# Last five groups of heads in two visits, their weights parked in DRAM, MLP operands made inside the attention

## Chip, cores, metric

One core of a Trainium2 chip. The metric is the device time of one execution in microseconds. All data is float32; matrix products are made of float32r parts (a high part, and a low part that is the rest).

## The reference

```python
x = A_x                                               # 1 x 2048 x 576
mod = (silu(c) @ w_mod)                               # six rows of 576: sa, ca, ga, sb, cb, gb
h = layernorm(x) * (1 + ca) + sa
# attention: 32 query heads of 128, 16 key/value groups, the last 512 cached positions
q = (h @ wq); p = softmax(q @ k.T * 128 ** -0.5); o = p @ v
x = x + ga * (o @ wo)                                 # wo: 4096 x 576
h = layernorm(x) * (1 + cb) + sb
gate, up = h @ W_gate, h @ W_up                       # 576 x 4608 each
x = x + gb * (((gate * (gate > 0)) * up) @ W_down)
```

## The kernel before

The 2048 tokens are four blocks of 512 (`qb` 0 to 3), kept transposed in `hT`. The attention runs over 128 **units**. A unit is one query head on one block of tokens: `unit(u)` gives group `g`, block `qb` and head; a group of two heads takes eight units in a row (four blocks by two heads), with the group's keys and values (`ks`, `vs`) and the heads' `wqs` and `wos` in SBUF.

In unit `u` the scores (`s_half`, L408 to L410) are followed on TensorE by the query projection of the next unit (`qproj`, L361), by `spread` (L436), by a piece of the output product (`piece`, L537), by the two halves of probabilities times values of the unit before (`pv_half`, L510 to L512), and by another piece. VectorE (DVE) reduces the scores to a maximum (L413, L421), adds up the exponentials' sums of the unit before (`sum_pre`, L428), broadcasts the maximum (L466), subtracts it (L483), broadcasts the inverse sum (L446), makes the low part of the next query (`q_lo`, L392) and scales the unit's output (`o_mul`, L518). ScalarE (ACT) makes the exponentials (L485), their high parts (L472), the high parts of outputs and weights, and copies the running sum into PSUM and back (L570, L546). GpSimd (POOL) makes the low parts of the exponentials (`lo_half`, L492, two per unit), their sums over keys (`ksum_op`, L498 and L501, three instructions per unit), the low part of the output (`o_lo`, L526) and of weights (`split`, L176). `spread` sends maximum and sum in one matmul, so it needs both L422 and L428.

All engines issue in the order in which the program is written. Work beside the units is put at a time by `step(name, t, fn)`: `t` is ten times the unit plus a place in it, and `run(u, k)` issues what is due at place `k` of unit `u` (`PLAN` adds a shift to some names, `CFG` picks engines of a layernorm). `prep` puts the load of a weight, its gate (`wo` is multiplied by the row `ga`, L216 on DVE) and its split at such times. `prep_mod` adds up the modulation rows (L127 on DVE).

`LayerNorm` takes a block of 512 tokens: statistics on DVE, scaling on ACT, transposes on TensorE (L306), an affine step, and for the MLP (`key == "b"`) a store to DRAM (`hb`). The MLP works on two halves of 1024 tokens (`b` 0 and 1), 18 blocks `m` each, in a scheme with seven products in place of eight: P1 to P7 with sums of weights (`wop`) and of tokens (`hop`: B11, B21, T1 to T4, B22). `w_prep` makes the weights of the first half and keeps them in DRAM (`wkeep`), from which the second half loads them. `md_piece` is the down product (L537), `ln_half` the second half's layernorm inside the first half's blocks, `h_later` its token operands, kept in `hkeep` and loaded by `h_back`. The first half's layernorms (`b0`, `b1`), token operands (`h_steps`) and first weights are made at the end of the attention, at times from `e - 41` to `e + 4`, where `e` is the end of unit 127.

Of the kernel before, what the change touches and what calls it, by code (L numbers as in the profile page):

```python
# [26 lines left out]
PLAN = {'a1.st0': -14, 'a1.nm0': -15, 'a1.st1': -14, 'a1.nm1': -15, 'a1.st2': -14, 'a1.nm2': -15, 'a1.st3': -14, 'a1.nm3': -15, 'a1.rs': -15, 'a1.tr0': -15, 'a1.af0': -11, 'a1.tr1': -15, 'a1.af1': -15, 'a1.tr2': -15, 'a1.af2': -15, 'a2.tr2': -1, 'wo2.g': 2, 'a3.st0': -10, 'a2.st2': -10, 'wq2.c': 4, 'wo2.l': -2, 'wo2.c': -2, 'mods': -3, 'k1.l': -5, 'k1.c': -8, 'gb': -12}  # L27
CFG = {'a3': (('m', 'aav', 'vap'), ('w', 'vvv', 'aav'), ('w', 'vvp')), 'a2': (('m', 'aav', 'vvv'), ('w', 'vvv', 'vvv'), ('s', 'aap')), 'a0': (('s', 'vvp', 'vvv'), ('m', 'aap', 'avp'), ('w', 'aav')), 'a1': (('w', 'aap', 'vap'), ('m', 'vvp', 'vvv'), ('s', 'avp'))}
PE0, PE1, MLP0 = 4, 3, 8


@with_exitstack
def kernel(
# [96 lines left out]
    def prep_mod(j, t):  # L130
        st = {}

        def load():
            st["raw"] = rp.tile([P, 640], F32, tag="raw", name=f"wm{j}_{t}")
# [71 lines left out]
    def prep_out(d, k, src, key, slot=None, at=(None, "wC")):  # L206
# [11 lines left out]
        def cut():  # L218
            raw = st["gated"]
            w = d[slot] = wp.tile([P, 2, D], F32R, tag=at[1], name=f"wo{key}_{k}")  # L220
            split(raw, D, w[:, 0, :], w[:, 1, :])
# [11 lines left out]
    def hb_store(qb, d, cols, f):  # L233
        if d < 4:
            nc.sync.dma_start(hb[qb, d][:, cols], f)
            return
        for j in range(2):
            s = f[32 * j:32 * j + 32]
            nc.sync.dma_start(hb[qb, 4][j, :, :, cols].rearrange("r p n -> p r n"),
# [17 lines left out]
    class LayerNorm:  # L257
        def __init__(self, qb, key, where):
            self.qb, self.key, self.where = qb, key, where
            self.xn, self.ps, self.ready, self.n = {}, {}, 0, 0  # L260
# [21 lines left out]
        def norm(self, i):  # L282
            pool, tag, w = self.where[i]
            n = pool.tile([P, w], F32, tag=tag, name=f"xn{self.key}_{self.qb}_{i}",
                          **({"bufs": 2} if tag == "lo" else {}))
            a = acc[4 * self.qb + i]
            act = dict(bias=self.rs[:, 1, i:i + 1], scale=self.rs[:, 0, i:i + 1])
            nc.scalar.activation(n[:, :512], a[:, :512], AF.Identity, **act)
            nc.scalar.activation(n[:, 512:640].rearrange("p (r n) -> p r n", r=2),
                                 a[:, None, 512:].to_broadcast([P, 2, 64]), AF.Identity, **act)  # L290
            self.xn[i] = n
            assert adds[4 * self.qb + i] == (HQ // 2 if self.key == "b" else 0)

        def trans(self, ds, pool, tag):
            nm = f"lt{self.key}_{self.qb}_{ds[0]}"
            if tag == "w":
                flush()
            if tag != "mm":
                t = pool.tile([P, 2, 512], F32, tag=tag, name=nm)
            for j, d in enumerate(ds):  # L300
# [4 lines left out]
                for i in range(4):  # L305
                    nc.tensor.transpose(self.ps[d][:, i * P:(i + 1) * P],  # L306
                                        self.xn[i][:, d * P:(d + 1) * P], ident)

        def affine(self, ds, pool, tag, engs):
            qb = self.qb  # L310
            if self.key == "b":
                add, mul = mods["b"]
                for d, e in zip(ds, engs):
# [7 lines left out]
                    hb_store(qb, d, slice(0, 512), f[:n])  # L321
                return
            if not self.ready:
                hT[qb] = [hp.tile([P, 512], F32R, tag="hT", name=f"hT{self.key}_{qb}_{k}")
                          for k in range(9)]
            h = hT[qb]
            self.ready += len(ds)
# [36 lines left out]

    NU = HKV * NQB * 2
    wqs, ks, vs, wos = {}, {}, {}, {}
# [3 lines left out]
    def unit(u):  # L370
        g, r = divmod(u, 2 * NQB)
        qb, hh = divmod(r, 2)
        return g, qb, 2 * g + hh
# [154 lines left out]
    def down_piece(his, los, ws, i, qt, nm, pool=None, seed=None):  # L528
# [3 lines left out]
        for half in range(2):  # L532
            cs = slice(half * H2, (half + 1) * H2)
            n = 0
            for hi, lo, w in zip(his, los, ws):
                for a, b in ((hi, 0), (hi, 1), (lo, 0)):
                    nc.tensor.matmul(ps[:, half, :H2], a[:, sl], w[:, b, cs],  # L537
# [68 lines left out]
    def order(m):  # L606
        return ("P1", "P6", "P2", "P7", "P5", "P4", "P3") if m else ("P1", "P2", "P6", "P7", "P5", "P4", "P3")
# [15 lines left out]
    def lay_steps():  # L623
        out = []
        for f in range(0, NFT, 2):
            for xx, src in enumerate((wg, wu)):
                for j in range(2):
                    out.append((wlay[f:f + 2, j, :, xx, 0:256], src[f:f + 2, :, 256 * j:256 * j + 256]))
        for f in range(0, NFT, 9):
# [696 lines left out]
```

## Time and profile before

| | |
|---|---|
| median of three runs | 3063.35 us (3063.14 to 3064.06) |
| profiled execution | 3058.63 us, span 3056.8 us, mean granted clock 0.982 |
| busy | PE 95%, PEld 83%, DVE 66%, POOL 65%, ACT 44% |
| DMA | 360.28 MB, mean 118 GB/s |

PE is TensorE's matmuls, PEld its weight loads, SP the engine that issues most of the DMAs. In a row of the timeline stand start, length, engine, line, operation, what is written and read, shapes, and in brackets the engine's idle time ahead of it and what ended it. "x2" is two instructions in one row. The slices are 40 equal parts of the span, in tenths.

### The profile page before, as it was taken

What the parts mean: (1) busy time and instruction counts of PE and PEld (TensorE: products, weight loads), DVE (VectorE), ACT (ScalarE), POOL (GpSimd) and SP (SyncE); (2) the same over time, 40 slices, a digit from 0 to 9 for tenths busy, and PEclk for the clock granted to TensorE, in tenths of its full rate; (3) what the DMA queues carried; (4) which work ended last, traced back from release to release, by engine and by line L of the source; (5) the groups of instructions that cost most, each with busy time, mean ns of one, the idle gap of its engine ahead of it and who ended that gap; (6) DMA issues with size and microseconds to landing.
All of it is one profiled execution on the core that took longest, in us unless ns stands there. A gap on an engine that the chain in (4) does not pass through costs nothing. (4 is left out here: it accounts for less than half of the span.)

```text
span 3056.8 us, 40707 instructions
## 1 busy us (share of the span) xinstructions
PE 2914.2 (95%) x15414; PEld 2533.1 (83%) x15414; DVE 2027.2 (66%) x2810; ACT 1360.2 (44%) x1875; POOL 1988.1 (65%) x1386
## 2 busy tenths in 40 slices
PE   6899999999999999999987699999999999999999
PEld 4688888888888888888875488888878888888888
DVE  7777777777777777777765656566767444444444
ACT  5566666666666666666653233333323111111110
POOL 5789899998998999898975556666666311111111
PEclk9999999999999999999998799999999999999999
DMA  4101111211111100000003256567777944444443
GB/s 146 39 23 50 66 62 63 73 58 55 47 43 51 34 24 28 16 16 21 25 29 99 107 210 218 212 222 273 267 273 252 346 162 161 162 164 162 175 161 116
DMA packets 143651, 360.28 MB, mean 118 GB/s; under 512 B 12768, under 2 KB 52448, under 8 KB 143456
## 3 DMA queue, kind: packets, MB, share of 16 engines
q1 hardware_dynamic: 115312, 245.15, 24.4%
q10 hardware_dynamic: 28144, 112.54, 9.3%
q8 instruction: 122, 2.00, 0.3%
q14 instruction: 73, 0.60, 0.1%
HBM read 234.62 MB, written 151.32 MB: 126 GB/s over the span
## 5 line engine op out<-in xcount | busy, mean ns | idle before, releaser
L492 POOL TENSOR_TENSOR lo<-p,hi 128x1024 fp32r<-128x1024 f32 x256 | 610.1, 2404 | 0.1
L864 PE MATMUL gu<-hop_T,wop 128*128 128x512 f32 (+1 forms) x2016 | 507.1, 396 | 18.3 <-ACT hop_T L714 11.1
L537 PE MATMUL md<-wogb,hhi 128*128 128x288 f32 x2304 | 477.0, 299 | 40.3 <-ACT lflh L849 16.2
L548 DVE TENSOR_TENSOR acc<-md,acc 128x576 f32<-128x576 f32 x288 | 217.5, 755 | 408.3 <-PE md L537 408.1
L413 DVE TRANSPOSE_TENSOR_REDUCE t<-s 128x32 f32<-128x1024 f32 x256 | 319.2, 1248 | 226.2 <-PE s L410 212.7
L537 PEld LDWEIGHTS md<-wogb,hhi 128*128 128x128 f32 x2304 | 389.3, 191 | 71.1 <-DVE acc L548 20.7
L864 PEld LDWEIGHTS gu<-hop_T,wop 128*128 128x128 f32 (+1 forms) x2016 | 372.7, 190 | 91.1 <-ACT hop_T L714 12.0
L537 PE MATMUL wo<-woga,ohi 128*128 128x288 f32 x2048 | 428.6, 302 | 13.2 <-DVE acc L548 8.5
L361 PE MATMUL qps<-hTa,wA 128*128 128x512 f32 x1792 | 431.8, 392 | 4.7 <-POOL hTa L349 3.5
L361 PEld LDWEIGHTS qps<-hTa,wA 128*128 128x128 f32 x1792 | 338.4, 189 | 76.5 <-POOL hTa L349 4.4
L501 POOL TENSOR_TENSOR ks<-ks,p 128x512 f32<-128x512 f32 x256 | 340.4, 1330 | 79.7 <-ACT p L485 65.2
L864 PE MATMUL gu<-hop_B,wop 128*128 128x512 f32 (+1 forms) x1512 | 382.9, 396 | 4.7 <-DVE hop_B L718 3.6
L537 PEld LDWEIGHTS wo<-woga,ohi 128*128 128x128 f32 x2048 | 333.6, 190 | 26.7 <-DVE acc L548 10.1
L880 POOL TENSOR_TENSOR hlo<-r,hhi 128x512 fp32r<-128x512 f32 x72 | 100.8, 1400 | 384.8 <-issue 240.8
L537 PE MATMUL md<-wogb,hlo 128*128 128x288 f32 x1152 | 343.6, 298 | 0.6 <-POOL hlo L880 0.6
L864 PEld LDWEIGHTS gu<-hop_B,wop 128*128 128x128 f32 (+1 forms) x1512 | 281.8, 191 | 62.3 <-DVE hop_B L718 4.0
L537 PE MATMUL wo<-woga,olo 128*128 128x288 f32 x1024 | 302.8, 296 | 0.1
L483 DVE TENSOR_TENSOR p<-s,mb 128x1024 f32<-128x1024 f32 x242 | 285.0, 1219 | 3.8
L472 ACT CAST hi<-p 128x1024 fp32r<-128x1024 f32 x256 | 269.2, 1052 | 8.0
L485 ACT ACTIVATE p<-p 128x1024 f32<-128x1024 f32 x242 | 255.5, 1056 | 5.5 <-POOL kv L176 4.9
L879 ACT CAST hhi<-r 128x512 fp32r<-128x512 f32 x72 | 44.7, 621 | 416.8 <-DVE r L889 334.9
L537 PEld LDWEIGHTS md<-wogb,hlo 128*128 128x128 f32 x1152 | 219.6, 191 | 1.4 <-POOL hlo L880 1.4
(180 smaller groups left out, 5292.9 us busy)
## 6 DMA issues: line engine op xcount, KB each, us to landing
wk_P<-wop ACTq DMA_DIRECT2D x126, 640.0 KB
wop<-wk_P SPq DMA_DIRECT2D x126, 640.0 KB
wr<-wlay SPq DMA_DIRECT2D x72, 384.0 KB
dk<-wogb ACTq DMA_DIRECT2D x36, 576.0 KB
wogb<-dk SPq DMA_DIRECT2D x36, 576.0 KB
rogb<-wd SPq DMA_DIRECT2D x36, 288.0 KB
rwA<-wq SPq DMA_DIRECT2D x32, 320.0 KB
wlay<-wg SPq DMA_DIRECT2D x36, 256.0 KB
```

Of the source, the lines that this page charges most:

```text
L361: return [lambda i=i, a=a, b=b: nc.tensor.matmul(ps, a, b, start=(i == 0), stop=(i == n - 1)) for i, (a, b) in enumerate(ops)]
L413: nc.vector.tensor_reduce(t4[u][:, 2 * h:2 * h + 2, :].rearrange("p k b -> p (k b)"), t.rearrange("p k (b j) -> p (k b) j", j=32), axis=AX ...
L472: nc.scalar.copy(hi_[u, h], pt[u, h])
L483: nc.vector.tensor_tensor(p, t, bc[u][:, None, :].to_broadcast([P, 2, 512]), op=ALU.subtract)
L485: nc.scalar.activation(p, p, AF.Exp, bias=0.0, scale=1.0)
L492: nc.gpsimd.tensor_sub(lo_[u, h], pt[u, h], hi_[u, h].bitcast(F32))
L501: nc.gpsimd.tensor_tensor(ks_[u], ks_[u], p[:, j, :], op=ALU.add)
L537: nc.tensor.matmul(ps[:, half, :H2], a[:, sl], w[:, b, cs], start=(n == 0 and seed is None), stop=(n == 5), skip_group_check=seed is not None)
L548: nc.vector.tensor_tensor(av, ps[:, :, :H2], av, op=ALU.add)
L864: nc.tensor.matmul(ps, a, c, start=s not in ("P2", "P3") and i == 0, stop=i == len(ops) - 1, skip_group_check=True)
L879: nc.scalar.copy(hi, r)
L880: nc.gpsimd.tensor_sub(lo, r, hi.bitcast(F32))
```

## The change

- The units are listed: groups 0 to 10 as before, then groups 11 to 15 with blocks 0 and 1 (units 88 to 107), then the same groups with blocks 2 and 3 (units 108 to 127). Pieces of the output product keep their regular times up to the end.
- The weights of groups 12 to 15 are split during groups 1 to 8 (`parks`) and stored in DRAM (`keep`, issued by ACT). Those of group 11 are stored after their first use. `again` loads them for each visit; every other odd `wo` is kept in two `raw` buffers.
- The first of the three sums of a unit goes from POOL to DVE, behind `q_lo`; `lo_half(u, 0)` stands right after the exponentials, and the other two sums stand after the copy of the high part.
- Splits of the groups' weights get new times (-30, -20, -14, 0, 20, 34 from the visit's begin `B`).
- The layernorms `b0` and `b1` run in units 108 to 117 with buffers of `hp`; the token operands of the first half are made in units 114 to 126 (`h0_load`, `h0_comb`, `h0_cut`), kept in `hkeep` and loaded by `h_back`.
- The seven weights of block 0 are made in units 24 to 84 on POOL (`w_later`) and loaded like those of the second half.
- `ln_half` transposes two and two columns in place of four; in `w_prep` the next block's loads are issued behind its own work; modulation rows go through the pool `xm`; the entries of `PLAN` and `CFG` for the layernorms `a2` and `a3`, the second group's weights and `gb` go.

```diff
-PLAN = {..., 'mods': -3, 'k1.l': -5, 'k1.c': -8, 'gb': -12}
+PLAN = {..., 'mods': -3}
+NLAST = 5
...
+    def keep(key, t):
+        akeep[key] = k = dr.tile(list(t.shape), F32R, name="ak%s%d" % key)
+        nc.scalar.dma_start(k.bitcast(F32), t.bitcast(F32))
...
+    VIS = [(g, (0, 1, 2, 3)) for g in range(HKV - NLAST)]
+    VIS += [(g, (0, 1)) for g in range(HKV - NLAST, HKV)] + [(g, (2, 3)) for g in range(HKV - NLAST, HKV)]
+    UNITS = [(g, qb, 2 * g + hh) for g, qbs in VIS for qb in qbs for hh in range(2)]
...
             ks_[u] = xp.tile([P, 512], F32, tag="xm", name=f"ks{u}")
-            nc.gpsimd.tensor_tensor(ks_[u], p[:, 0, :], p[:, 1, :], op=ALU.add)
+            nc.vector.tensor_tensor(ks_[u], p[:, 0, :], p[:, 1, :], op=ALU.add)
...
+        if m % NFP == 0 or m >= NFP:
+            nc.sync.dma_start(w_tile(n).bitcast(F32), wkeep[m % NFP, s].bitcast(F32))
             return
...
+    def h0_cut(s, x, t):
+        a, n = h0[(*x, t)], 96 if t == 2 else P
+        hi = hp.tile([P, 512], F32R, tag="hT", name=f"hy0_{s}_{t}")
+        nc.scalar.copy(hi[:n], a[:n])
+        if t < 2:
+            lo = hp.tile([P, 512], F32R, tag="hT", name=f"hz0_{s}_{t}")
+            nc.gpsimd.tensor_sub(lo, a, hi.bitcast(F32))
...
+    H = 10 * UNITS.index((HKV - 1, 1, HQ - 1))
+    norm_steps("b0", 0, "b", None, None, (H + 16, H + 20, H + 26, H + 29), H + 30,
+               (H + 34, H + 36, H + 44, H + 46), (H + 48, H + 58, H + 68), (H + 49, H + 59, H + 69), www)
...
+            for (key, d, pr), t in zip(weights(g, live), (-30, -20, -14, 0, 20, 34)):
+                prep(key[0] + str(key[1]), B + t, pr, 3)
...
+        for c, t in (("q", 10), ("kv", 26), ("o", 44)):
+            if parks[c]:
+                key, d, pr = parks[c].pop(0)
+                prep("park", B + t, pr, 3)
+                sk(B + t + 9, key, d, key[1])
...
         exp_half(u, 0)
-        ksum_op(u, 0)
         flush()
         run(u, 5)
         exp_half(u, 1)
-        ksum_op(u, 1)
+        lo_half(u, 0)
         if u:
             sum_bc(u - 1)
...
             piece(at[10 * u + 6])
+        ksum_op(u, 0)
         run(u, 7)
...
         flush(pend_act)
-        lo_half(u, 0)
+        ksum_op(u, 1)
         lo_half(u, 1)
         run(u, 9)
```

More of the change, by code (lines that the diff above doesn't have):

```diff
@@ new lines @@
+    parks = {c: [w for g in early for w in weights(g, {x: {} for x in "qkvo"}) if w[0][0] in c]
+             for c in ("q", "kv", "o")}
+    seen, first = {0}, HKV - NLAST
+    for i in range(1, len(VIS)):
+        g, qbs = VIS[i]
+        B = 10 * UNITS.index((g, qbs[0], 2 * g))
+        if g in early or g in seen:
+            for key, t in zip((("q", 2 * g), ("k", g), ("q", 2 * g + 1), ("v", g), ("o", 2 * g),
+                               ("o", 2 * g + 1)), (-30, -20, -14, 0) + ((-4, -4) if i > first + 1 else (6, 34))):
+                step("again", B + t, again, key, live[key[0]], key[1],
+                     key[0] == "o" and key[1] % 2 and i > first and (i - first) % 2 == 0)
+        else:
+            for (key, d, pr), t in zip(weights(g, live), (-30, -20, -14, 0, 20, 34)):
+                prep(key[0] + str(key[1]), B + t, pr, 3)
+                if any(v[0] == g for v in VIS[i + 1:]):
+                    sk(B + t + 12, key, d, key[1])
+        seen.add(g)
@@ L1107 @@
             mat(2 + 2 * i, s, fn)
-    later = [fn for s in TERMS for t in range(3) for fn in h_later(s, t)]
+    later = [fn for s in TERMS for t in range(3) for fn in h_later(1, s, t)]
     for i, fn in enumerate(later):
@@ L1149 @@
     mlp = mlp_slots()
-    def hs(names):
-        for name in names.split():
-            h0[name]()
     def last_unit():
```

390 lines of the change are left out of this document (215 added, 175 removed).

## Prediction

> **What bounds the kernel now.** I read the page's shares first, then busy time by stretches, then one unit of the attention engine by engine.
>
> ```profile
> span 3056.8 us, 40707 instructions
> PE 2914.2 (95%) x15414; PEld 2533.1 (83%) x15414; DVE 2027.2 (66%) x2810; ACT 1360.2 (44%) x1875; POOL 1988.1 (65%) x1386
> PE   6899999999999999999987699999999999999999
> PEclk9999999999999999999998799999999999999999
> ```
>
> TensorE is busy 95% of the span. It is short of work at the start and in slices 20 to 23, between attention and MLP, where the granted clock falls too. Stretches of time put a size on that (first column the length, then PE busy and its matmuls; PEclk is the third figure from the end):
>
> ```profile
> 1039.00:1051.08 12.08, 12.08 (x66) 10.55 (x65) 10.12 (x14) 7.88 (x11) 11.60 (x7) 1.00 0.15 47
> 1551.75:1781.70 229.95, 170.61 (x791) 139.24 (x790) 144.90 (x191) 83.10 (x122) 127.00 (x99) 0.87 0.29 100
> 2440.30:2475.58 35.28, 35.28 (x195) 31.23 (x194) 16.12 (x21) 4.09 (x6) 5.18 (x4) 1.00 0.51 172
> ```
>
> The first row is one steady unit, the third one block of the MLP: 66 matmuls in 12.08 us and 195 in 35.28 us, 0.183 and 0.181 us each. At 0.182 us the 791 matmuls of the crossing would take 144 us. It takes 230, so 86 us are lost there: 59 us of idle PE (229.95 - 170.61), the rest matmuls stretched by the clock of 0.87. PE waits for operands made only then, for instance (last figures: idle before, and on whom):
>
> ```profile
> L864 PE MATMUL gu<-hop_T,wop 128*128 128x512 f32 (+1 forms) x112 | 32.9, 438 | 16.9 <-ACT hop_T L714 11.1 <-DVE hop_T L718 2.6 <-DVE hop_T L720 1.7
> ```
>
> Now a steady unit, the stage that the change touches most. PE rows L436 are the `spread` that each unit's softmax hangs on:
>
> ```profile
> 1213.38 0.35 PE L436 MATMUL qm<-t,quad 128*128 128x80 f32 x2
> 1225.46 0.35 PE L436 MATMUL qm<-t,quad 128*128 128x80 f32 x2
> 1209.04 2.61 DVE L413 TRANSPOSE_TENSOR_REDUCE t<-s 128x32 f32<-128x1024 f32 x2 [2.20 <-PE s L410]
> 1212.13 0.70 DVE L428 TRANSPOSE_TENSOR_REDUCE t<-ks 128x16 f32<-128x512 f32 x1
> 1214.77 2.36 DVE L483 TENSOR_TENSOR p<-s,mb 128x1024 f32<-128x1024 f32 x2
> 1217.67 0.65 DVE L392 SCALAR_TENSOR_TENSOR qlo<-qps,qhi 128x512 fp32r<-128x512 f32 x1
> 1218.24 0.67 DVE L518 TENSOR_TENSOR rb<-pv,rb 128x512 f32<-128x512 f32 x1
> 1209.14 0.63 ACT L546 COPY acc<-wo 128x576 f32<-128x576 f32 x1
> 1217.81 1.06 ACT L472 CAST hi<-p 128x1024 fp32r<-128x1024 f32 x1
> 1218.76 1.06 ACT L485 ACTIVATE p<-p 128x1024 f32<-128x1024 f32 x1
> 1230.30 1.05 ACT L472 CAST hi<-p 128x1024 fp32r<-128x1024 f32 x1
> 1208.30 2.67 POOL L501 TENSOR_TENSOR ks<-ks,p 128x512 f32<-128x512 f32 x2 [0.70 <-ACT p L485]
> 1210.93 4.75 POOL L492 TENSOR_TENSOR lo<-p,hi 128x1024 fp32r<-128x1024 f32 x2
> ```
>
> The unit is 12.08 us (1225.46 - 1213.38), set by PE. `spread` needs L428, which adds up the sums L501 made on POOL. Those sums end at 1210.97, 1.2 us before L428 reads them, because POOL makes them ahead of the two `lo` (L492, 2.4 us each). DVE has 2.2 us idle ahead of L413.
>
> **The change part by part.** *The crossing.* Layernorm of the first 1024 tokens, the seven hop operands and the seven wop of block 0 are made earlier, so block 0 finds them in DRAM. What stays: in the last unit no query projection covers the softmax, some 3 us, and the last `lo`, sum and output product, a few us. I leave 4 of the 86 us: -82, bounds -86 (nothing stays) and -50 (loads of the operands late, below). The 40 transposes stay work.
>
> *A unit with nothing extra.* The first sum goes from POOL to DVE, behind `q_lo`; on POOL `lo_half(u, 0)` now runs ahead of the sums. DVE reaches the sum at 1218.3, POOL's `lo` can start when L472 ends, at 1218.87. So DVE is first, takes about 0.7 us (free row of L216 below), and eats a third of its 2.2 us. POOL: `lo` 1219.0 to 1221.4, two sums of 1.33 to 1224.1. L428 must start 0.87 us before the next `spread` (its 0.70, and 0.17 to PE, two rows below), at 1224.59: a margin of 0.5 us. In the next unit ACT is 0.4 us later against PE (L472 at 1230.30, 12.49 after 1217.81) and the margin is 0.2 to 0.3. So 0 us, but of the 1.2 us that L428 had, next to nothing is left; its cover is this margin alone, and 0.3 us lost in each of some 115 units would be +35.
>
> ```profile
> 68.97 0.70 DVE L428 TRANSPOSE_TENSOR_REDUCE t<-ks 128x16 f32<-128x512 f32 x1
> 69.84 0.34 PE L436 MATMUL qm<-t,quad 128*128 128x80 f32 x2
> L176 POOL TENSOR_TENSOR wA<-rwA,wA 128x640 fp32r<-128x640 f32 x24 | 38.0, 1582 | 0.0
> L176 POOL TENSOR_TENSOR kv<-rkv,kv 128x512 fp32r<-128x512 f32 x25 | 35.8, 1434 | 0.0
> ```
>
> *Splits at step 6 of a unit.* `run(u, 6)` now stands between `lo_half(u, 0)` and the sums, so a split there delays L428. The second query weight of groups 1 to 11 comes at B-14, eight key or value weights at B+26. 11 x (1.58 - 0.5) + 8 x (1.4 - 0.5) = 19 us; I take 17. Before, such splits stood behind the sums. Bounds 0 (margin larger than I think) to 28 (no margin). Splits at step 4 of the tighter units push the exponential's copy instead: 11 x 0.4 = 4.
>
> *Gates, and the port of DVE and POOL.* L216 multiplies two SBUF operands on DVE. It is free in the first row, and behind POOL's work in the others:
>
> ```profile
> 129.37 0.72 DVE L216 TENSOR_TENSOR roga<-roga,mrow 128x576 f32<-128x576 f32 x1
> 1142.16 1.64 DVE L127 SCALAR_TENSOR_TENSOR macc<-wm,sT,macc 128x576 f32<-128x576 f32 x1
> 1140.78 2.41 POOL L492 TENSOR_TENSOR lo<-p,hi 128x1024 fp32r<-128x1024 f32 x1
> 1143.14 1.81 POOL L176 TENSOR_TENSOR kv<-rkv,kv 128x512 fp32r<-128x512 f32 x1
> 2104.14 3.15 DVE L216 TENSOR_TENSOR rogb<-rogb,mrow 128x576 f32<-128x576 f32 x1
> 2104.15 1.27 POOL L659 TENSOR_TENSOR wop<-wr,wop 128x512 fp32r<-128x512 f32 x1
> 2105.39 1.28 POOL L794 TENSOR_TENSOR hxB<-hxB,hyB 128x512 fp32r<-128x512 f32 x1
> ```
>
> L127 waited for `lo` (to 1143.19), ended 0.61 us later, and POOL's next ran 1.81 us instead of 1.43. 30 gates (22 of groups 1 to 11, eight parked) come behind the output product, now at 1219.65, when `lo` has just begun: the gate ends at 1221.4 + 0.6 = 1222.0. L413 to the end of L428 takes 3.79 us (1209.04 to 1212.83), so `spread` comes at 1226.0 instead of 1225.46: 0.5 us, and 0.9 in the other units. 30 x 0.7 = 21 us, bounds 0 and 30. [...]
>
> *Modulation sums* (15, L127, ahead of L483): in even units DVE then reaches the sum as `lo` may start (0.1 us apart), and the loser waits 2.4 us, some 1.9 us of PE. Half of 8 x 1.9, and 7 x 0.3: 10 us, bounds 2 and 25.
>
> *wop of block 0 in units 24 to 84* (14 on POOL, 384 columns, 1.0 us a combination by L501's 1.33 for 512): ten have a piece at step 6, four of them 2 us with a copy on ACT between. 12 us, bounds 5 and 25. The stores of kept weights take ACT's queue 0.33 us each, mostly in its idle time (1.95 us ahead of the query's copy): 0 to 3, taken 1.
>
> ```profile
> L617 ACTq DMA_DIRECT2D wk_P<-wop x126: 326/327/360, 1663.4 to 2394.6; - x126
> 1213.58 0.60 ACT L388 ACTIVATE qhi<-qps 128x512 fp32r<-128x512 f32 x1 [1.95 <-PE qps L361]
> hop_T<-hkT SPq DMA_DIRECT2D x16, 256.0 KB
> ```
>
> *Layernorms in the attention.* Each of six transposes now waits in PE's queue for the copy L546 of the piece before it (behind the exponential that ends at 1219.82, 0.63: to 1220.5, where PE was free at 1219.5), and then runs itself:
>
> ```profile
> 75.52 1.04 PE L306 MATMUL lta<-ident,xna 128*128 128x128 f32 x8
> ```
>
> 4 x (0.95 + 1.04) + 2 x 1.45 = 11 us; the statistics and the scaling 5 more. Bounds 8 and 25.
>
> *Hop operands in the last twenty units.* 12 combinations on DVE, each like a gate or at a worse place (1.0), and 21 splits on POOL (1.3), eight of them ahead of the sums (0.8 with the margin): 18 us, bounds 5 and 35. No weights are split there any more, which is why not more.
>
> *Later groups from DRAM, start, MLP.* The visits of two blocks load 3.4 MB (two query, key, value and output weights with their low parts, by tile sizes) per four units (48 us), 71 GB/s, against 330 GB/s reached at 2400 to 2450: 0. The hand-set times of the second and third layernorm go, and DVE gets the sums in the start:
>
> ```profile
> 42.00:145.00 103.00, 80.13 (x355) 63.71 (x356) 81.84 (x135) 54.87 (x78) 75.13 (x53) 0.90 0.10 31
> 2400.00:2450.00 50.00, 48.43 (x269) 42.20 (x268) 20.70 (x28) 6.34 (x9) 7.77 (x6) 1.00 0.92 330
> 1803.19 0.54 PE L537 MATMUL md<-wogb,hhi 128*128 128x288 f32 x2 [2.80 <-ACT lflh L849]
> ```
>
> 355 matmuls at 0.182 are 65 us of these 103, so DVE and ACT decide there: +4, bounds -10 and +20. In the MLP the four-column transposition is cut in two; the 2.8 us wait gets about 1 us shorter but comes once more, four times: +3, bounds -8 and +8.
>
> **Sum.** -82 + 17 + 4 + 21 + 10 + 12 + 1 + 16 + 18 + 4 + 3 = +24. From the profiled execution's 3058.6 us that is 3083; the median of the runs shown (3063.35) stands 4.7 us above it, so 3087 us.
>
> **Rivals.** *The stalls are hidden and the kernel gets faster.* One mechanism: the sums reach L428 earlier than I place them, so that the unit takes up a late DVE or POOL. My 64 us of splits, gates, modulation and wop are some 90 events of 0.7 us; below 0.45 each the change gains. If the margin takes up most of them (10 us left) and half of the 34 for layernorms and hop operands, 3087 - 54 - 17 = 3016 us. For it: the sums were 1.2 us early before, and DVE had 2.2 us idle. Against it: `lo` now stands ahead of the sums. *Every unit gets longer*: POOL's `lo` gets the port before DVE's sum; DVE waits 2.4 us, the loop from `spread` to `spread` gets near 12.4 us: 115 x 0.3 = 35 on top, 3120 us. For it: the margin of 0.2 us; against: DVE is 0.5 us ahead. *The crossing stays*, as the change doesn't do what it says: the last hop loads (four of 1.2 MB, five tiles like the row above, 15 us at 330 GB/s) and weights stand in one SP queue behind buffers that attention still holds, and block 0 waits as before for half of the loss, 3087 + 32 = 3119. For it: these loads stand behind each other on SP; against: the first slots need only the early ones. *POOL passes DVE over repeatedly*, as at 2104.14: then a gate ends behind three more POOL instructions, +5 us each, 150 in all: 3235.
>
> **How the numbers follow.** My forecast (3068 to 3108) has 0.46, the faster rival 0.33 (2995 to 3060), longer units 0.10, the crossing 0.08, the last 0.03. A change of 0.2% (6 us) is about what a measurement can tell here. Within it lie the edges of the first two, 0.08; faster 0.31, slower 0.61. The range 3012 to 3126 leaves 0.1 of the rival below and 0.1 above.
>
> **What would show it.** Units of 12.08 us with nothing extra, and 12.6 to 14 us with a gate, a step-6 split or a wop piece, PE waiting at `spread` for the sum on DVE; the new DVE sum at 0.7 us, gates at 2.3; the crossing within 5 us of its matmuls, its clock near 1. I am wrong if most units with a gate or split keep 12.08 (then faster), if clean units are longer, or if PE waits for hop loads in block 0.

## The result, and the profile after

The changed kernel takes 3152.74 us (median of four, 3142.96 to 3153.76) against 3063.6: 1.0284 times as long, 95% interval 1.0263 to 1.0304. The direction was as forecast. The size wasn't: 89 us instead of 24, and 27 us beyond the upper end of the range.

The page after, the span and TensorE's lines:

```profile
span 3150.3 us, 41269 instructions
PE 2939.7 (93%) x15414; PEld 2535.5 (80%) x15414; DVE 2131.5 (68%) x2925; ACT 1361.2 (43%) x1885; POOL 1859.4 (59%) x1294
PE   6799989988999999999888989999999999999999
PEclk9999999999999999999999999999999999999999
```

The hole of slices 21 to 23 is filled, and digits of 8 stand now in the attention (slices 6, 9 and 10), in its last units (20 to 22) and in the MLP (24). Cutting the span at the starts of `spread` and of a block's first `gu` matmul shows where the 93.5 us of the two profiled spans went:

| stretch (us) | before | after | difference |
|---|---|---|---|
| up to unit 8 | 168.4 | 171.0 | +2.7 |
| units 8 to 95 | 1069.2 | 1165.2 | +96.0 |
| units 96 to 107 | 145.0 | 145.0 | 0.0 |
| units 108 to 121 | 169.2 | 211.3 | +42.1 |
| unit 122 to block 2 | 230.0 | 153.6 | -76.4 |
| blocks 2 to 9 | 308.3 | 331.8 | +23.5 |
| blocks 10 to 18 | 350.3 | 355.8 | +5.5 |
| the rest | 616.5 | 616.6 | +0.1 |

Five of these stretches of the changed kernel (units 8 to 95, unit 96, units 108 to 121, the crossing, blocks 2 to 9), columns as in the prediction:

```profile
171.02:1336.17 1165.15, 1099.22 (x5657) 939.49 (x5656) 920.72 (x1281) 724.40 (x982) 929.03 (x570) 0.98 0.24 80
1336.17:1348.25 12.08, 12.08 (x65) 10.55 (x64) 9.33 (x14) 7.11 (x9) 8.54 (x6) 1.00 0.12 43
1481.13:1692.43 211.30, 184.24 (x937) 153.82 (x936) 159.48 (x237) 120.10 (x166) 145.68 (x94) 0.98 0.33 113
1692.43:1846.07 153.64, 142.94 (x747) 122.11 (x747) 103.27 (x139) 65.25 (x91) 95.95 (x66) 0.99 0.56 191
1846.07:2177.86 331.79, 299.66 (x1594) 261.74 (x1593) 187.92 (x240) 101.43 (x149) 186.57 (x178) 0.96 0.57 204
```

A unit with nothing extra still takes 12.08 us, all twelve of units 96 to 107. In units 8 to 95 TensorE idles 66 us (1165 - 1099), and its own work takes longer too: 1099.22 us against 1067.67 in the kernel before, whose row follows, at a mean clock of 0.98 against 1.00.

```profile
168.36:1237.54 1069.18, 1067.67 (x5654) 931.25 (x5652) 821.22 (x1185) 707.52 (x946) 972.25 (x595) 1.00 0.15 49
```

The wait that grew is the one of `spread` for the sum on DVE. Waits of TensorE, first before, then after (total, times, longest):

```profile
PE qm L436 <- DVE t L428: 8.1, 4, 2.6
```

```profile
PE qm L474 <- DVE t L466: 77.2, 55, 6.6
```

**A load that stands in SP's queue.** Waits of 6 us weren't in the forecast. One of them in the timeline (ends of unit 27; L840 and L849 are `w_later`'s combination and copy, L829 its loads, L213 the load of a parked output weight, L217 its gate, L451 and L466 the unit's maximum and sum):

```profile
414.53 1.01 POOL L840 TENSOR_TENSOR wx_P<-wx_P 128x384 f32<-128x384 f32 x1
415.57 0.33 SPq L829 DMA_DIRECT2D wx_P<-wlay  x1
416.63 1.06 SPq L213 DMA_DIRECT2D roga<-wo  x1
426.18 2.40 DVE L217 TENSOR_TENSOR roga<-roga,mrow 128x576 f32<-128x576 f32 x1 [6.33 <-DMA roga<-wo]
428.50 2.37 DVE L451 TRANSPOSE_TENSOR_REDUCE t<-s 128x32 f32<-128x1024 f32 x2
432.11 0.71 PE L474 MATMUL qm<-t,quad 128*128 128x80 f32 x2 [6.59 <-DVE t L466]
SPq L829 <- POOL wx_P L840: 17.1, 2, 12.0
409.00:416.00 7.00, 6.08 (x33) 5.04 (x32) 5.42 (x10) 1.37 (x4) 6.92 (x6) 1.00 0.03 9
```

The third term's load overwrites what POOL's combination reads, so SP stands for 12.0 us until that has ended (415.54). The DMA engines are all but idle (9 GB/s), though the output weight's load stands next in line. It starts at 416.63, right behind two others, and the gate that waits for it starts 9.5 us later. On DVE the gate stands ahead of the unit's maximum, and so `spread` comes 6.59 us late. Unit 27 takes 19.06 us. Five gates wait for such a load, four of them 6.3 to 7.2 us, 28.5 us in all:

```profile
DVE roga L217 <- DMA roga<-wo: 28.5, 5, 7.2
```

**In the MLP** TensorE's down product waits for ScalarE's affine step of the transposed columns: twice per half layernorm before, three times after, and twice again with four columns in one transposition (e3_ln_four, below). In that order:

```profile
PE md L537 <- ACT lflh L849: 16.2, 8, 2.8
```

```profile
PE md L575 <- ACT lflh L900: 32.1, 12, 4.2
```

```profile
PE md L575 <- ACT lflh L900: 16.3, 8, 2.8
1842.53:2150.79 308.26, 292.01 (x1594) 255.83 (x1592) 185.74 (x240) 101.41 (x149) 188.56 (x178) 0.99 0.63 219
```

The three waits of one half layernorm after, with ScalarE ahead of the third, then the two in e3_ln_four:

```profile
1951.21 0.53 PE L575 MATMUL md<-wogb,hhi 128*128 128x288 f32 x2 [2.32 <-ACT lflh L900]
1959.82 0.53 PE L575 MATMUL md<-wogb,hhi 128*128 128x288 f32 x2 [1.52 <-ACT lflh L900]
1968.12 0.67 ACT L176 CAST wogb<-rogb 128x576 fp32r<-128x576 f32 x1 [1.26 <-DVE rogb L217]
1968.69 0.56 ACT L900 ACTIVATE lflh<-ltlh,mcol,mcol 64x256 f32<-64x256 f32 x1
1969.30 0.85 PE L575 MATMUL md<-wogb,hhi 128*128 128x288 f32 x2 [4.18 <-ACT lflh L900]
```

```profile
1940.30 0.53 PE L575 MATMUL md<-wogb,hhi 128*128 128x288 f32 x2 [2.78 <-ACT lflh L900]
1948.44 0.54 PE L575 MATMUL md<-wogb,hhi 128*128 128x288 f32 x2 [1.27 <-ACT lflh L900]
```

The first wait did get shorter, from 2.78 to 2.32 us. The second pair adds one of 1.52. Most of the growth is in the last column, whose wait goes from 1.27 to 4.18 us. With two pairs ahead of it, it comes one place later in the block, and there its affine step stands on ScalarE behind the copy of a gated weight (L176), which waits for DVE's gate.

### The profile page after: what moved, and what is told of

The parts are those of the page before. It is cut to its first block, busy times and chain, and to the rows that moved or that the text cites. A ratio compares the mean times of both kernels' runs of the same rounds, so it can differ in the third digit from the quotient of the medians.

```text
span 3150.3 us, 41269 instructions
## 1 busy us (share of the span) xinstructions
PE 2939.7 (93%) x15414; PEld 2535.5 (80%) x15414; DVE 2131.5 (68%) x2925; ACT 1361.2 (43%) x1885; POOL 1859.4 (59%) x1294
## 5 line engine op out<-in xcount | busy, mean ns | idle before, releaser
L530 POOL TENSOR_TENSOR lo<-p,hi 128x1024 fp32r<-128x1024 f32 x256 | 623.2, 2435 | 314.4 <-ACT hi L510 281.1
L575 PE MATMUL md<-wogb,hhi 128*128 128x288 f32 x2304 | 480.7, 301 | 52.7 <-ACT lflh L900 32.1
L451 DVE TRANSPOSE_TENSOR_REDUCE t<-s 128x32 f32<-128x1024 f32 x256 | 314.0, 1239 | 131.7 <-PE s L448 122.3
L374 PE MATMUL qps<-hTa,wA 128*128 128x512 f32 x1288 | 311.8, 393 | 8.7 <-ACT lfa L356 4.9
L575 PE MATMUL wo<-woga,ohi 128*128 128x288 f32 x1472 | 313.6, 306 | 5.0 <-ACT wo L608 3.5
L374 PEld LDWEIGHTS qps<-hTa,wA 128*128 128x128 f32 x1288 | 244.1, 190 | 61.8 <-ACT lfa L356 5.3
L575 PEld LDWEIGHTS wo<-woga,ohi 128*128 128x128 f32 x1472 | 244.0, 193 | 15.4 <-ACT wo L608 5.2
L575 PE MATMUL wo<-woga,olo 128*128 128x288 f32 x736 | 220.3, 299 | 0.0
```

Of the source, the lines that this page charges most:

```text
L374: return [lambda i=i, a=a, b=b: nc.tensor.matmul(ps, a, b, start=(i == 0), stop=(i == n - 1)) for i, (a, b) in enumerate(ops)]
L451: nc.vector.tensor_reduce(t4[u][:, 2 * h:2 * h + 2, :].rearrange("p k b -> p (k b)"), t.rearrange("p k (b j) -> p (k b) j", j=32), axis=AX ...
L530: nc.gpsimd.tensor_sub(lo_[u, h], pt[u, h], hi_[u, h].bitcast(F32))
L575: nc.tensor.matmul(ps[:, half, :H2], a[:, sl], w[b][:, cs], start=(n == 0 and seed is None), stop=(n == 5), skip_group_check=seed is not None)
```

## The experiments

The kernel before stood between 3064 and 3069 us beside the different runs, so the ratios are compared; 0.001 is 3 us. Stretches are those of the table, from the profiled executions. Unless said otherwise an edit is made in the changed kernel, and the result stands against its 1.0284.

**The splits at step 6.** e1_lo_late puts `lo_half(u, 0)` behind the sums:

```diff
         exp_half(u, 1)
-        lo_half(u, 0)
...
         ksum_op(u, 1)
+        lo_half(u, 0)
         lo_half(u, 1)
```

> The changed kernel with lo_half(u, 0) back behind the sums; the first sum stays on DVE. Theory (the sums that spread waits for now stand behind a 2.4 us lo on POOL, so a split at step 6 or a gate makes the unit late): splits at step 6 and gates fit into the unit again; of the 96 us that units 8 to 96 lost some 35 to 45 come back, units of groups without parked weights take 12.08, and the time is near 3110 us. Rival (the sum on DVE is what costs, by its port with POOL): no more than 10 us come back, 3140 to 3150 us.

1.0229 [1.0213, 1.0244]. Units 8 to 95: 1142.4, 22.8 us less. That lies between the theory's 35 to 45 and the rival's 10, and near the forecast's 17 + 4, though the edit takes away part of the gates' cost as well (units 9 and 17 go from 12.53 to 12.08, as they do without gates in e5 below; 11 such units make 5 us). e4_place0 leaves the order and moves the splits from step 6 to step 0 of the next unit:

```diff
-            ... zip(weights(g, live), (-30, -20, -14, 0, 20, 34)):
+            ... zip(weights(g, live), (-30, -20, -10, 0, 20, 34)):
-        for c, t in (("q", 10), ("kv", 26), ("o", 44)):
+        for c, t in (("q", 10), ("kv", 30), ("o", 44)):
```

> The changed kernel with the 19 splits of step 6 at step 0 of a unit (B-10 in place of B-14, B+30 in place of B+26), so that they stand ahead of the unit's output low part and not between lo and the sums. Theory (each of them costs about 1 us through the late sums): 15 to 20 us less, near 3134 us; the seventh unit of each group, 12.9 us now, takes 12.1. Rival (POOL's load counts, not its order): within 6 us of 3151.

1.0247 [1.023, 1.0264], units 8 to 95 9.9 us less, below the theory's 15 to 20. The lengths of units 80 to 87 (differences of successive starts of `spread`) show both edits where only a group's own weights are split:

```
after        12.86 12.62 12.21 12.44 12.17 12.08 12.91 12.17
e4_place0    12.90 12.62 12.22 12.45 12.17 12.08 12.08 12.08
e1_lo_late   12.08 12.08 12.08 12.09 12.08 12.08 12.10 12.51
```

The 0.83 of the seventh unit is the second query weight's split ahead of the sums. For a parked key or value weight it is 1.03 in the third unit of six groups (unit 18: 13.22 to 12.20). 11 x 0.83 + 8 x 1.03 make 17 us, the forecast's number; the whole edit brings less, as units with `w_later` pieces get longer by it (unit 55 by 4.5).

**The gates.** e5_no_ga leaves out the multiplication by `ga` (L216, L217 in the changed kernel):

> Leaves out the multiplication of the output weights by their gate row in the attention (32 instructions on VectorE); the waits and transfers stay. The forecast gave the gates 21 us (30 x 0.7). Theory from the units of the changed kernel: a unit with a gate and no w_later piece is only 0.1 to 0.5 us longer, so some 9 us come back, about 3143 us. Rival, the forecast's size: 21 us back, 3131 us. Rows with a slow third load (18 to 19 us for one unit) stay, since the wait for the weight moves from the gate to the copy.

1.0191 [1.017, 1.0212]: units 8 to 95 25.5 us less, some 28 in all. My theory (9 us) fell, the forecast's 21 was the better number. I had read it off rows of a group with two gates. But 18.0 of the 25.5 us come from units 27, 35, 43 and 51, whose gates wait for the load behind SP (part of it returns in units 30, 40 and 55, which get 10.7 longer). Where no `w_later` piece stands, e5 brings 2.2 and 2.6 us in the two groups of units 8 to 23, and 0.7 and 0.4 in those of units 80 to 95, which have no parked weight. From these rows I estimate 8 x 2.4 + 3 x 0.6, 21 us for the gates alone, the forecast's number. Beside a parked weight a gate counts more: unit 17 goes from 12.53 to 12.08, 18 from 13.22 to 12.65, 19 from 13.19 to 12.46.

**SP's queue alone.** e2_sp_free loads the third term at the start, into a slot of its own:

```diff
-            for x, term in zip("ab", terms):
+            for x, term in zip("abh", terms):
                 get(st[x], *term[1:])
+        def fourth():
+            get(st["b"], *terms[3][1:])
...
-            x, y = st["a"], st["b"]
+            x, y = st["a"], st["h" if i == 2 else "b"]
```

> The changed kernel where the third operand of a block-0 weight is loaded at the start into the space of the high part, and the fourth by a step of its own, so that SP no longer waits for POOL's combination with the load of a parked output weight behind it. POOL's work is the same. Theory (the gate on DVE waits for that load, 28.5 us in five waits): units 24 to 64 lose some 28 us less, and DVE's wait for roga is near 0: near 3122 us. Rival (POOL's combinations at step 6 are what costs there): within 8 us of 3151.

1.0228 [1.0213, 1.0243], units 8 to 95 18.3 us less, not the theory's 28; unit 27 takes 13.93 instead of 19.06. Units 29 and 37, to which the edit moves the fourth term's combination, get 8.8 us longer (16.02 and 17.26), so the chain is worth more than 18. What is left of DVE's wait for these loads:

```profile
DVE roga L217 <- DMA roga<-wo: 2.4, 3, 1.7
```

**The wop operands of block 0.** e13_wl_only moves them to units 70 to 107, into buffers of the pool `xm`, each load in a step of its own. The modulation's sums and columns get other times with it, and the row `gb` waits in DRAM:

```diff
-            w = wp.tile([P, 1280], F32, tag=tag, name=f"wx_{s}_{xx}")
+                st[x] = xp.tile([P, 640], F32, tag="xm", name=f"wx{x}_{s}_{xx}")
...
+    T = 700
+    for s, xx in longs + shorts:
+        for k, fn in enumerate(w_later(s, xx)):
+            step("w.l", T, fn)
...
-        prep(f"m{3 + i // 5}.{i % 5}", 104 + 50 * i, prep_mod(3 + i // 5, i % 5))
+        prep(f"m{3 + i // 5}.{i % 5}", 104 + 40 * i, prep_mod(3 + i // 5, i % 5))
```

> The wop operands of block 0 alone are moved from units 24 to 84 to units 70 to 107, with buffers of their own kind and each load in a step of its own after the combination that frees its buffer; the modulation steps that these buffers collide with come every 40 instead of every 50 and the gate row of the MLP waits in DRAM. The sums stay as in the changed kernel. The forecast gave these operands 12 us. Theory: they cost 42 us where they stood, because SP's queue and the gate wait behind their third load, and 5 to 10 at the new place: 32 to 37 us back, 3116 to 3121 us at the reference's 3064. Rival: their cost overlaps that of the splits at step 6 (undoing these gave 23), so less than 20 come back, above 3133 us.

1.022 [1.0203, 1.0237], 20 us less: neither theory's 32 to 37 nor clearly the rival. With a spacing of 40 all modulation sums fell into units 2 and 6 of a group, behind the splits at step 6 (unit 18: 14.81 instead of 13.22; unit 22: 14.40 instead of 12.90). e17_wl_mods takes that out:

```diff
-        prep(f"m{3 + i // 5}.{i % 5}", 104 + 40 * i, ...)
+        prep(f"m{3 + i // 5}.{i % 5}", 134 + 80 * (i // 2) + 20 * (i % 2), ...)
```

> As e13_wl_only, with the modulation sums in units 5 and 7 of a group, where no weight is split at step 6. Theory: the wop operands cost 40 to 50 us where they stood and 5 to 8 at the new place, and the sums cost less in units 5 and 7 than before (0 to 0.3): units 8 to 96 lose 50 to 60 us instead of 102, median 3103 to 3110. Rival: the wop operands share their cost with splits and gates, which stay: at most 25 us back, 3128 us or more.

1.015 [1.0135, 1.0166], 41 us less, and 40 less in units 8 to 95. The window of these units, and what DVE waited for ahead of the gates (the line of `ga` in the same view; no load is left):

```profile
173.70:1299.01 1125.31, 1086.13 (x5657) 928.71 (x5655) 921.44 (x1281) 722.03 (x979) 920.63 (x561) 1.00 0.25 81
L229 DVE TENSOR_TENSOR roga<-roga,mrow x32: 745/2936/2957, 68.3 to 1230.5; 128x576 f32<-128x576 f32 x32
  ACT mrow L151: 1.2, 1
```

The edit moves the modulation sums too, so the 40 are not all the operands'. In units 26 to 70, where the operands stood, 42.0 us come back; leaving out sums brings 6.3 us there (e14, next). That leaves 36 to 42 us for the operands at the place the change gave them. Units 71 to 95, where most of them stand now, get 4.4 us longer, units 96 to 107 2.0. The rival (their cost is shared with splits and gates) fell by its number of 25, but four units (27, 35, 43, 51) gain in e5 as well, 18.0 us there and 22.4 here: that much is one chain, which either edit takes apart.

**Modulation.** e14_no_mod leaves out 12 of the 15 sums.

> Leaves out 12 of the 15 modulation sums on VectorE in the attention (all but the first of each of the three rows); loads stay. The forecast: 10 us for 15, 1.9 each in even units and 0.3 in odd ones, so 8 back. Theory: the rows of eight units that lose least (80 to 95) hold no such sum, rows 8 to 23 hold two or three and lose 2 to 3 us more, a part of it parked weights; 3 to 8 us back, 3145 to 3150 us. Rival: they stand on the path in every unit like a gate (0.75 each and the port's wait): 15 to 20 back, 3133 us.

1.024 [1.0224, 1.0255], units 8 to 95 12.4 us less: between theory and rival, above the forecast's 8 (10 for 15).

**Layernorms and hop operands.** e6_no_comb leaves out `h0_comb`; there are 12 of them, the 18 in the text is a slip.

> Leaves out the 18 combinations of hop operands of block 0 on VectorE in the last twenty units; loads, splits and stores stay. The forecast: a combination costs 1.0 us, so 18 us here with the 18 of them counted as 12. Theory now: these units wait for the copies and splits in ScalarE's and GpSimd's order, in which the combinations stand between two splits, so 12 to 20 us of the 42 + 20 lost in units 108 to 128 come back, 3130 to 3140 us. Rival: the first sum on VectorE, which in these units falls behind GpSimd's lo (2.33 us instead of 0.7), decides there; then at most 5 us come back, 3148 us.

1.0233 [1.0217, 1.0249]; 12.0 us less from unit 108 to block 2 (203.9 + 149.0). So it is theory's lower end, and 1.0 us for each. e9_no_hop leaves out the copies and subtractions too:

> Leaves out the combinations and the splits (copy on ScalarE, subtraction on GpSimd) of the hop operands of block 0 in the last twenty units; their loads and stores, and both layernorms, stay. The forecast: 18 us for the hop operands, 16 for the layernorms. Units 106 to 113, which stand before the first hop operand, already lose 19 us in the changed kernel, so theory: the layernorms are mis-sized, 30 to 35 us of the 58 lost in units 106 to 128 stay and 23 to 28 come back, 3122 to 3128 us. Rival: the hop operands are mis-sized, 40 or more come back, 3110 us.

1.0197 [1.0182, 1.0212], 23.8 us less in the same stretch (195.8 + 145.4), as the theory had it. Units 106 to 127 lose 58.3 us over 12.08 each in the changed kernel and 34.5 here. The last unit's 5.9 us is among them, and the kernel before has it, too (17.95 and 17.93). So the hop operands cost 24 us. The 29 that are left are put down to the layernorms as a remainder: no run leaves the layernorms out. What a layernorm does to a unit, in the changed kernel (units 110 and 111 take 16.2 and 19.4; the first row, a statistics step, stands on DVE ahead of the maximum for the `spread` of the second), and TensorE's waits over units 108 to 121 in e9, which has the layernorms without the hop operands:

```profile
1518.60 0.82 DVE L273 BATCH_NORM_STATS2 stb<-acc 128x6 f32<-128x288 f32 x2 [2.39 <-ACT acc L584]
1523.14 0.45 PE L474 MATMUL qm<-t,quad 128*128 128x80 f32 x2 [2.36 <-DVE t L466]
1532.83 1.97 PE L317 MATMUL ltb<-ident,xnb 128*128 128x128 f32 x8 [2.79 <-ACT acc L584]
1596.68 1.09 PE L317 MATMUL ltb<-ident,xnb 128*128 128x128 f32 x8 [0.79 <-ACT acc L584]
```

```profile
PE wo L575 <- ACT wo L608: 6.8, 8, 1.6
PE ltb L317 <- ACT acc L584: 5.6, 6, 1.7
PE qm L474 <- DVE t L466: 3.3, 2, 2.3
```

The forecast's form of a transposition was 0.95 us of waiting and 1.04 of work. Five of the six have it (the last row above is one; the two short ones run 0.66), only the one at 1532.83 is longer. In e9 the six wait 5.6 us and run 5.7, as forecast (11). What the forecast didn't have is the first row of the waits: the output product waits for ScalarE's copy of the running sum into PSUM (L608). An example from the changed kernel, where the layernorm's scaling (L297) stands on ScalarE ahead of that copy:

```profile
1559.94 0.81 ACT L297 ACTIVATE xnb<-acc,rsb 128x512 f32<-128x512 f32 x1
1563.06 0.64 ACT L608 COPY wo<-acc 128x576 f32<-128x576 f32 x1
1563.75 0.54 PE L575 MATMUL wo<-againo,ohi 128*128 128x288 f32 x2 [1.59 <-ACT wo L608]
```

e10_ln_mm gives the transpositions other PSUM buffers:

```diff
-    www = (("w", "aap", "vvp"), ("w", "aap", "vvp"), ("w", "aap"))
+    www = (("m", "aap", "vvp"), ("m", "aap", "vvp"), ("m", "aap"))
```

> The six transpositions of the layernorm inside the attention go to PSUM buffers of the kind mm, one for each column, so that they no longer flush ScalarE's copies of the output product and don't wait for them. Forecast: 0.95 us for each such wait, 6 us in all; the wait rows of the changed kernel say 6.7 us over six. Theory: 5 to 8 us back, 3146 us. Rival: these buffers are the ones of the query projection and of the product with the values, which then wait instead: no change or up to 10 us longer.

1.0262 [1.0245, 1.0279], 8.6 us less in units 108 to 121. The transposes' waits were on the path.

**The MLP.** e3_ln_four transposes four columns at once again, in a buffer `wC`:

```diff
-                f = hp.tile([P, 2, 256], F32, tag="hT", name=f"lf{nm}_{ds[0]}")
+                f = wp.tile([P, 4, 256], F32, tag="wC", name=f"lf{nm}_0")
...
-        return [stats, norm, lambda: trans((0, 1)), lambda: trans((2, 3)), lambda: trans((4,))]
+        return [stats, norm, lambda: trans((0, 1, 2, 3)), lambda: trans((4,))]
```

> The changed kernel with ln_half as before: four columns transposed at once. Theory (the transposition in two halves makes TensorE wait once more for ACT's copy, in each of four MLP blocks): blocks 2, 4, 6 and 8 take 41 to 42.6 us again in place of 46.6 to 49.3, 23 us less, near 3128 us. Rival (those blocks are slower because of DMA traffic or of hp's buffers): they stay above 45 us and the time within 8 us of 3151.

1.0208 [1.0192, 1.0223], 23 us less; blocks 2 to 9 take 308.3 as before, as the theory had it. The edit also takes the columns out of `hp`'s buffers; ScalarE's affine step didn't wait for these in the changed kernel (no idle time ahead of its 20 instructions there, its semaphore waits take 38 ns at most), so that part of the rival finds no support in the trace. The kernels that keep the two pairs show 327.5 to 331.8 there, so the price is 19 to 23.5 us.

**Together.** e7_moved is e1, e3 and e13:

> Three steps undone or moved together: lo_half(u, 0) back behind the sums, four columns in one transposition in the MLP, and the wop operands of block 0 made in units 70 to 107, in buffers of their own kind, with each load in a step of its own after the combination that frees its buffer. Theory: 23 + 23 us as measured for the first two alone, of which some overlap, and about 42 us of the w_later pieces come back less 10 to 15 for their new place: 3150 - 23 - 23 - 30 = 3074 us, still above 3063. Rival: the pieces cost the same wherever they stand: 3105 us.

1.0033 [1.002, 1.0046], units 8 to 95 1104.2; the theory's 3074 us (1.0033). e8_sum_pool has the first sum on GpSimd again, ahead of the two `lo`:

> As e7_moved, and the first sum is back on GpSimd in the order of the kernel before, ahead of the lo. Theory: in the attention the same time as e7_moved within 5 us, and in units 108 to 128, where the sum on VectorE stands behind the lo (2.33 us instead of 0.7), 10 to 20 us less: 3055 to 3065 us. Rival: GpSimd, with three sums and two lo per unit, has no room for the splits at step 6 and for the hop splits: 10 to 30 us more than e7_moved.

1.0028 [1.0016, 1.0039]. The same time; units 108 to 121 got no shorter (213.5), so theory fell there. Units 3 and 7 of a group still lost 1.6 and 0.4 (1.3 to 2.0 and 0.5 to 1.0 in e8), so the moves of e4 were added to both:

> e7_moved, and the second query weight's split moves from step 6 of the seventh unit of a group to step 0 of the eighth, the parked key or value weight's from step 6 of unit 2 to step 0 of unit 3. In e7_moved units 3, 6 and 7 of a group are 1.6, 0.8 and 0.4 us longer than 12.08. Theory: the 0.8 and part of the 1.6 go, 10 to 15 us in all, about 3065 us by the time of the kernel before at 3064 (ratio 1.000). Rival: the split costs the same at its new step: ratio 1.003.

> e8_sum_pool with the same two moves. There units 3 and 7 of a group are 1.7 and 0.75 us longer: GpSimd has 10.05 us of its own work in a unit of 12.08, so that one split of 1.4 fits and two don't. Theory: with one split in a unit less is lost, 10 to 15 us in all, ratio 0.999. Rival: two splits now meet in unit 3 (key or value weight at step 0, output weight at step 4): unchanged, ratio 1.003.

With the sum on VectorE 0.998 [0.9971, 0.9989], 0.2% less than the kernel before and better than the theory; with the sum on GpSimd 1.0022 [1.0012, 1.0031]. In the latter unit 3 still takes 13.9 (13.4 with the sum on VectorE): two splits of 1.4 don't fit beside 10.05 us of POOL's own work. e15_all and e16_all_kv add e10's buffers and another place for the third modulation's column; e15 also moves the parked key or value weight to unit 7:

> e11_moved_place, and three more: the layernorm's transpositions in PSUM buffers mm (8.6 us less in units 108 to 122 by e10_ln_mm), the column of the third modulation at unit 29 instead of 27 beside a gate (4 to 5 us), the parked key or value weight's split from unit 3 to step 4 of unit 7, where no gate stands (unit 3 loses 1.3 in eight groups: up to 8 us, less what unit 7 then loses). Theory: the losses stand in different units and add up: 15 to 20 us, ratio 0.992 to 0.993. Rival: unit 7 with two splits loses what unit 3 gains, and the mm buffers hold the query projection: ratio 0.996 to 0.998.

> As e15_all with the parked key or value weight's split left at step 0 of unit 3. Theory: 3 to 8 us more than e15_all. Rival: 0 or less, if the two splits of unit 7 cost as much there.

e15: 1.005 [1.0035, 1.0065]. Theory and rival both missed: unit 7 stays at 12.35, but the unit after it takes 15.3 to 18. A row of unit 32 tells why:

```profile
482.57 0.62 ACT L188 CAST kv<-rkv 128x512 fp32r<-128x512 f32 x1 [7.18 <-PE pv L562]
```

The split's buffer is the one from which the products with the old group's values still read, and ACT stands 7.18 us with all its copies behind it. e16, without that move, is the fastest, and its theory (3 to 8 us more than e15) fell, too: 3047.59 us, 0.9943 [0.9928, 0.9958]. Its units 8 to 95:

```profile
172.39:1259.09 1086.70, 1074.38 (x5657) 930.25 (x5656) 884.93 (x1281) 725.14 (x979) 912.89 (x561) 1.00 0.25 84
```

12 us of idle TensorE are left there instead of 66. e18_all_mods puts e16's sums in units 5 and 7 of a group:

> e16_all_kv with the modulation sums in units 5 and 7 of a group. There a unit with such a sum loses 0.3 (12.63 against 12.34). Theory: 2 to 4 us less, ratio 0.993. Rival: the sums take VectorE's time beside the weights of units 5 and 7: unchanged, ratio 0.994 to 0.995.

0.9969 [0.9959, 0.9979]; unit 2 of a group, which held a sum, mostly falls from 12.63 to 12.08, and unit 5 stays below 12.2 but for unit 69 (13.91), but the columns of the third and fourth modulation now make units 29 and 47 16.2 and 17.6 long. The theory fell: slower than e16.

## Why the prediction missed

By its own terms (a price is that of the edit that takes the item out, in the stretch where it stands):

| term | forecast | measured | from |
|---|---|---|---|
| crossing | -82 | -87 | 153.6 - 230.0, less the 10.3 that units 122 to 126 lose over 12.08 each |
| splits at steps 6 and 4 | 21 | 23, 5 of it the gates' | e1; by the units of e4 17 at step 6 |
| gates | 21 | 25, with part of SP's chain | e5; 21 by units without that chain |
| modulation | 10 | 12 for 12 of 15 | e14 |
| wop of block 0 | 12 | 36 to 42 | e17, e14 |
| layernorms in the attention | 16 | 29 | remainder of e9 |
| hop operands | 18 | 24 | e9 |
| start | 4 | 3 | table |
| `ln_half` | 3 | 19 to 23 | e3 |
| blocks 10 to 18 | none | 5 | table |

The measured column adds up to 89 to 99 us for the 93.5 of the spans. That is no proof that the terms are apart: units 27, 35, 43 and 51 are paid in e5 and in e17, 0.45 us of each group's second unit in e1 and in e5, and some edits make other units longer. A price holds beside what else stands there. The crossing's -87 lies past the bound of -86 because the 40 transposes left it (791 matmuls before, 747 after); the prediction kept them there as work and counted their time in the layernorms' term again. The time of its last rival is a slip as well: 3087 + 150 is 3237, not 3235. The stores' 1 us has no measurement. Right were the splits and the gates, unit by unit, and a clean unit at 12.08 us, with DVE's new sum ahead of POOL's `lo` and as short as forecast (the first two rows; their order turns in busy units, as in the last two):

```profile
1341.04 0.67 DVE L536 TENSOR_TENSOR ks<-p 128x512 f32<-128x512 f32 x1
1341.72 2.41 POOL L530 TENSOR_TENSOR lo<-p,hi 128x1024 fp32r<-128x1024 f32 x1 [3.46 <-ACT hi L510]
1608.46 2.39 POOL L530 TENSOR_TENSOR lo<-p,hi 128x1024 fp32r<-128x1024 f32 x1 [1.73 <-ACT hi L510]
1609.07 2.33 DVE L536 TENSOR_TENSOR ks<-p 128x512 f32<-128x512 f32 x1
```

Right were also the gate as an instruction (2.3 us forecast):

```profile
L217 DVE TENSOR_TENSOR roga<-roga,mrow x32: 745/2520/2954, 67.1 to 1267.9; 128x576 f32<-128x576 f32 x32
```

and the crossing, whose waits for hop operands are gone. The rival of hidden stalls fell; so did the one of longer units, the one of a crossing that stays, and the one of gates that POOL passes over repeatedly (2.95 us at most). No run shows the port of DVE and POOL by which the forecast explains waits of gates and modulation sums; what the runs show is the gates' length, 0.75 to 2.95 us with a median of 2.52 in the row above.

The steps that failed are three, by these prices 53 to 63 of the 66 us that were missing:

- *wop of block 0, 12 us, bounds 5 to 25.* The sum took POOL's time and a copy on ACT. It didn't ask what is queued behind the loads on SP, though the loads were counted for the later groups. The third load waits for POOL, a gate's load waits behind it, and the gate stands ahead of the maximum on DVE. e2 puts at least 18 of the 36 to 42 us on that chain. Copies of `w_later` also stand in ScalarE's order and wait for POOL (its waits, the changed kernel):

```profile
ACT wx_P L849 <- POOL wx_P L840: 37.0, 8, 6.6
```

How much of the rest is theirs was not measured.
- *`ln_half`, 3 us, bounds -8 to 8.* The sum had the first wait 1 us shorter and once more the same. By the rows above the two pairs wait 2.32 + 1.52 in place of 2.78, 1.1 us more per half layernorm, 4 us over four: near the forecast. It had nothing for the last column. That moves one place later in the block, behind ScalarE's copy of a gated weight, and waits 2.9 us more each time, 12 us over four. The other 8 of the 23.5 are TensorE's own work at a lower clock (last section). No run moved the last column alone, so this division is read from the trace; that undoing the whole step brings 19 to 23 us is shown.
- *Layernorms in the attention, 16 us, bounds 8 to 25.* The 11 us for the transposes were right (5.6 of waiting and 5.7 of work in e9). The 5 us for statistics and scaling were not: some 17 of the 29 are outside the transposes. The sum left out that the scaling stands on ScalarE ahead of the running sum's copy, for which TensorE waits 6.8 us in e9, and statistics on DVE stand ahead of a maximum while they wait for the output product's copy (2.39 us at 1518.60); `spread` waits 3.3 us for DVE. The other 7 us are not accounted for one by one.

Still open is the 5.5 us of blocks 10 to 18; other kernels with the change show 352.4 to 358.3 there.

## What to carry to other kernels

A load that waited for a free buffer held the loads behind it in SP's queue for 12.0 us here, so a moved step is priced with the queues it passes through, and its loads get a step of their own, after what frees the buffer. Count each engine's work per period and put extra pieces one to a period, away from the others: here nearly the same work cost 89 us in one set of places and gained 18 us over the kernel before in another. A step split in two moves what comes behind it: here the pair's second wait cost 1.1 us, and the column that came one place later 2.9.

## What the runs showed of the hardware

The 6.59 us wait of unit 27 was paid twice, since the matmuls behind it took longer, too. The output product's two matmuls in a steady stretch and behind that wait:

```profile
414.17 0.43 PE L575 MATMUL wo<-woga,ohi 128*128 128x288 f32 x2
432.55 0.83 PE L575 MATMUL wo<-woga,ohi 128*128 128x288 f32 x2
```

The granted clock (third figure from the end) over 4.8 us from the start of a `spread`: in a steady unit, after that wait, after a wait of 2.21 us (end of unit 10), and after one of 2.24 us (end of unit 50):

```profile
1336.17:1340.97 4.80, 4.80 (x29) 4.30 (x28) 4.38 (x7) 3.25 (x5) 2.09 (x2) 1.00 0.00 0
432.11:436.91 4.80, 4.80 (x19) 4.56 (x20) 4.02 (x7) 1.01 (x2) 1.65 (x2) 0.56 0.35 108
210.16:214.96 4.80, 4.80 (x20) 4.44 (x21) 4.28 (x7) 2.75 (x5) 3.61 (x3) 0.64 0.00 0
748.42:753.22 4.80, 4.80 (x28) 4.25 (x29) 4.28 (x7) 3.18 (x6) 4.80 (x4) 1.00 0.16 48
```

In units 8 to 95 a `spread` that waited up to 1.9 us and the 25 matmuls behind its first take 4.7 to 4.8 us. After the one wait of 3.0 us they take 6.4, after the four of 6 us and more 6.6 to 7.4, and after 2.2 us once 4.8 and once 6.4. Behind the waits of 6.59, 2.21 and 3.02 us the granted clock stood at 0.50 for a time, in that order:

```profile
429.50:436.32 6.82, 4.21 (x16) 4.12 (x17) 5.91 (x11) 2.49 (x5) 3.72 (x4) 0.50 0.29 91
211.05:214.45 3.40, 3.40 (x13) 3.12 (x13) 3.37 (x4) 2.24 (x5) 2.21 (x3) 0.50 0.00 0
890.30:893.70 3.40, 3.40 (x15) 3.34 (x15) 3.08 (x5) 0.86 (x2) 3.18 (x3) 0.50 0.08 28
```

Of the waits of `spread` in these units, 2.21 us is the shortest behind which the trace has a lower clock; behind the one of 2.24 us it stayed at 1.00.

In blocks 2 to 9 the split transposition adds 15.8 us of waiting (32.1 - 16.3), and TensorE's busy time is 7.7 us longer as well (299.66 against 292.01, clock 0.96 against 0.99): together the 23.5. The forecast priced waits at their length only.
